# Two S4 convolutions mixed by a gate: fine magnitudes read by DVE from PSUM in every fifth table step instead of every third, in a new order

## The chip, the cores and the metric

The kernel runs on one core of one Trainium2 chip. A core has five engines that run at their own pace and meet at semaphores: PE (matrix multiplies), DVE (the vector engine), ACT (the scalar engine with its function tables), POOL (GpSimd, which cannot read PSUM) and SP, which issues transfers. The metric is the device time of one launch in microseconds; the time given is the median of three runs. A profile is one execution, recorded by the hardware, with its own time.

## The reference

The input `u` has 2048 positions and 512 channels. Two state-space layers A and B, each with 128 complex states per channel, turn it into two outputs, and a gate mixes them:

```python
g = sigmoid((x * gate_w).sum(-1, keepdims=True))
def layer(u, A_re, A_im, B_re, B_im, C_re, C_im, log_dt, Dskip):
    dt = exp(log_dt)[:, None]
    logdA, dB = dt * (A_re + 1j * A_im), dt * (B_re + 1j * B_im)
    P = exp(logdA[:, :, None] * l[None, None, :])          # 512 x 128 x 2048
    K = einsum("dn,dnl,dn->dl", C_re + 1j * C_im, P, dB).real
    y = irfft(rfft(u, 2 * L) * rfft(K, 2 * L))[:L] + u * Dskip
return g * layer_A(x) + (1 - g) * layer_B(x)
```

The sum over l of complex exponentials gives each channel a filter K of 2048 taps, and the layer is a causal convolution with it. Everything is float32.

## The kernel before, in words

The 512 channels are cut into 8 blocks of 64; with layers A and B side by side a block has 128 channel rows. The work has four parts.

*Preparation* (`prep`, `exp_dt`, `seed`, `seed_angles`): per state and channel the logarithm, the angle and the weight are worked out, and from these the *seeds*. The exponential over 2048 positions is split in two factors, fine and coarse, and each factor in two short lists: `ml` holds eight magnitudes for single positions (columns 0 to 7) and eight for steps of 8 (columns 8 to 15), `mh` the same for coarse steps, `sa` the angles as integers. ACT fills `ml` and `mh` with exponentials of the logarithm (line 523), once for each block; POOL makes the angles (lines 535 to 541).

*Tables* (`tables(T)`, 64 steps, T = 0 to 63, eight to a block, 16 channel rows each). A step has

- on POOL, the angles `ang`: two operations of 128x512 integers (lines 549 and 552);
- the *fine magnitudes*: `mr[:, :, 0:64]`, 128x1024, the outer product of the two halves of `ml` (lines 555 to 565). This is what the change is about;
- on POOL (or DVE), the *coarse magnitudes* `mr[:, :, 64:96]`, 128x512, from `mh` (line 566);
- on ACT, a sine of the angles, a sine of the half angles and a square (lines 570 to 572);
- on DVE, four products that turn these into the real and imaginary tables `mr` and `ei` (lines 573 to 579);
- on PE, 128 small multiplies, `kgen` (line 588), that sum over the states and give the filter's taps, and a copy into `kt` by ACT or DVE. Every second step adds the skip weight (POOL) and runs the first stage of the transform of the filter, `first` (line 605), with two copies into `xa` or `xb`.

In two of three steps the fine magnitudes are one operation on POOL, or on DVE where the order says so; both inputs are in SBUF. In the third, when `T % 3 == 2`, ACT first copies the eight seeds of each row (128x128) into a PSUM bank of the ring `c` (line 558), and DVE multiplies that by the other half of `ml` (line 559), so that one of its inputs comes from PSUM.

*Convolutions* (`conv`, `back`): for each block, eight times a second transform stage on PE (line 618) and a product with the transform of the input on DVE (line 690), and after every two of these an inverse stage on PE (line 710), two copies and a round trip through memory in another layout. *Finish* (`fin`): the last stage with the gate folded in (line 742), a copy, and a store.

All helpers record operations in a `Plan`; nothing is issued while they run. `ORDER` (lines 82 to 150) is a list, written out in the file, of the numbers of these operations: it sets in which sequence they are issued, and so each engine's queue. A number with `b` takes the second engine of those that an operation allows: DVE instead of ACT for a copy (`"act dve"`), DVE instead of POOL for an operation marked `any` (`"pool dve"`), POOL instead of SP for a store. Lines 269 to 298 are helpers that many operations share, so the profile has products under L271 and L281, activations under L284, copies under L294 (ACT) and L296 (DVE).

Buffers are rings: `mr` has three, `ang`, `ei` and `kt` two, `c` four PSUM banks; a ring's next buffer is the one whose last use stands earliest in the order. An engine that comes to an operation whose buffer is still in use waits, and everything behind it in its queue with it.

Of the kernel before, what the change touches and what calls it, by code (L numbers as in the profile page):

```python
# [82 lines left out]
6 7 11 8 9 4 2 182 3 1 82 83 0 84 475 86 186 183 18 19 20 24 21 22 23 25 26 27 28 29 30 31 32 33 34 35 37 88 184b 185b 38 17  # L83
36 85 190 326 40 44 45 39 41 42 46 47 48 366 76 49 50 51 59 79 73 71 75 187 52 53 188 189 54 55 56 57 138 58 191 193b 61 62
67 63 60 68 192 64 69 91 14 351 87 13 218 194 15 16 98 65 70 92 93 101 94 95 89 96 43 72 66 353 77 354 78 90 74 100 99 195
102 357 104 103 105 219 113 197b 196b 198 200 355 356 221b 114 360 358 359 199 201 385 203 205 386 361 107 204 206 106 220
226 127 222 327 202 207 210 213 208 209 211 212 129 80 97 12 368 369 383 367 81 10 384 362 108 363 109 110 111 215 214 370
364 216 365 223 112 116 115 371 224 373 122 121 117 123 374 225 372 388 124 118 119 120 387 375 227 217 1403 230 125 126 128
131 134 376 228 389 136 133 231 352 132 137 135 130 5 1406 229 429 232 377 233b 244 390 378 245 391 392 393 249 394 251 395
430 250b 397 398 399 400 401 246 402 403 479 247 477 476 480 478 141 396b 404 405 406 142 143 239 144 252b 145 146 248 1414  # L90
253 148 149 234 150 151 152 407 254 240 431 416 414 427 415 154 139 140b 153 235b 155 236 418 408 379 419 420 409 237 483 417
421 422 428 410 445 446 447 147 448 241 242 156 157 432 380 381 423 159 424 435 158 436 411 433 434 437 413b 438 382 412 160
458 459 481 255 262 175 238 258 484 449 450 257 256 425 439 161 163 452 451 426 440 485 460 482 441 461 162 259 165 166 260
261 453 172 171 173 174 454 263 462 463 265b 167 164 455 168 169 612 611 464 264 609 613 177 266 179 243 176 328 330 331 290
329b 465 267 269b 268b 466 456 457 610 487 467 468 280 282 281b 469 283b 488 470b 294 284 486 170 180 499 501 616 489 502 490
491 492 471 500 442 493 518 519 516 517 494 472 444 443 503 504 495 496 506 332 275 505 473 474 531 333 507 508 520 521 509
276b 497 510 498b 522 511 532 523 524 529 533 530 277 285 278 287 270 272 286 534 535 288 525 526 536 547 549 550 548 512 537
538 334 335 608 279 289 527 336 551 539 540 552 271 553 560 562 561 554 555 528b 541 337 273 564 542 513 563 556 339 178 338
557 558 579 514 515 567 568 580 565 559 566 581 577 543 578 582 593 591 592 594 1407 1408 569 570 585 1404 544 586 583 546
584 545 340 587 588 1405 595 596 341 571 572b 598 342 1415 1426 614 618 615 573 619 599 1416 597 1425 617 181 1417 1409 1410  # L100
1411 274 1412 589 633 590 622 623 349 345 1427 600 1418 1419 601 574 602 575 576 624 603 620 621 649 347 343 625 634 626 1420
1429 635 631 632 651 652 604 348 650 744 1421 636 637 681 1428 1436 1450 1437 1422b 627 1430 628 1438 639 640 605 629 638 607
606 630 653 1413 1423 1424 1447 1439 1431 654 641 642 655 1432 643 656 657 658 662 663 664 665 666 644 679 680 645 659 695
667 1433 668 1448 660 1440 669 670 1449 682 1441 684 685 661 683 693 671 672 687 344 350 694 696 346 646 647b 1442 688 1443b
1444b 1434 1458 741 742 746 648 686 673 1459 745 674 743 1451 1435 1445 1461 689 690 691 1460 1452 692b 712 710 675 711 713
676 697 698 700 1453 701 699 678 677 714 1454 715 1455 1462 702 1446 703 717 704 1757 1763 705 725 1463 718 726 716 1764 1758
1483 1469 1470 719 723 727 724 747 751 749 706 753 754 748 752 728 729 1464 720 1471 1465b 750 1759 1765 1456 1480 1472 1466b
721 1760 1766 731 1761b 876 730 732 733 722 1767 1481 1473 878 755 707 1482 734 1474 735 708 783 709 756 757 736 1762 1457
1768 1475 1484 764 766 765 737 767 758 784 759 760 768 1476 769 1477 738 761 771 1485 740b 739b 772 770 773 1491 1467 1494
1468 1478 1502 762 1486 1487b 1488b 774 1495 1496 877 874 875 1492 1503 1493 775 785 781 795 814 782 796 815 786 763 787 776  # L110
# [3 lines left out]
835 836 810b 837 850 811 1776 848 851 1779b 856 857 849 838 852 879 858 839 883 859 880 853 860 885 886 861 1528 1519 882  # L114
1501 854 1529 862 1520 855b 863 864 1521 1010 840 884 887 897 899 900 898 1780 1777 1522 842 841b 865 1530 866 1531b 1532b
888 889 291 292 890 867 868 293 891 892 901 295 893 894 297b 296 902 869 914 916 915 904 917 870 905 903 871 872 1538 1523
298 299 918 302 1533 1534 1512 906 895 301b 907 303 921 922 305b 908 927 928 919 300 920 896b 304b 929 932 933 909 316 306
308 923 924 930 307b 309b 931 945 946 947 910 318 1784 925 935 317b 1785b 936 926b 1781 1007 934 1008 319 1009 1011 1782 977
310 937 938 978 323 321 322b 939 1786 320 1783 324b 325 1535 1006 1546 948 949 952 940b 958 959 960 961 1014 941 979 950 313
311 1790 1787 951 953 312 314 1791 962 954 975 976 911 955 965 1788 963 966 913 964 912 1539 1536 956 1540 967 989 968 942  # L120
957 980 943 981 982 1537 944b 983 991 990 1547 1548 984 1550 1541 985 1542b 986 1543b 315 1015 1549 1571 1557 1789 969 1551
1558 987 1144 1143 970b 993 1016 1012 1013 992 971 994 1559 988 995 996 997 998 972 974 973 1552 1031 1017 1020 1553 999 1032
1018 1554 1544 1560 1582 1033 1019 1029 1000 1021 1001 1561 1023 1024 1562 1572 1002 1030 1003 1022 1034 1025 1026 1573 1037
1035 1036 1005 1004 1027 1569 1047 1049 1048 1050 1060 1038 1545 1555 1579 1568 1792 1139 1556 1028 1051 1052 1563 1564 1565
1039 1040 1054 1583 1041 1053 1042 1062 1061 1043 1063 1093 1077 1094 1055 1570 1574 1580 1064 1065 1056 1067 1057 1575b
1576b 1044 1068 1584 1581 1046b 1566 1590 1140 1141 1066 1069 1142 1045 1058 1591 1059 1079 1070 1080 1592 1091 1078 1081
# [3 lines left out]
1103 1128 1275 1182 1129 1606 1130 1131 1132 1802 1613 1602 1120 1803 1133 1603 1614 1134b 1150 1104 1151 1162 1163 1152 1135  # L130
1164 1165 1153 1156 1154 1105 1801 1615 1589 1155 1107 1106 1157 1183 1179 1180 1158 1136 1607 1166 1137 1167 1138b 1169 1159
1170 1225 1608 1609 1168 1600 1623 1637 1610 1271 1616 1160 1624 1617 1184 1226 1625 1171 1618 1185 1273 1172 1619b 1620 1635
1173 1187 1634 1804 1188 1161b 1186 1272 1174b 1636 1276 1274 1626 1621 1611 1193 1227 1194 1195 1175 1196 1210 1211 1627
1176 1189 1190 1628 1191 1197 1178b 1200 1198 1177 1199 1629 1192b 1630 1631 1638 1201 1622 1648 1645 1202 1639 1203 1646
1811 1212 1213 1214 1215 1216 1812 1640 1641 1632 1670 1647 1217 1218 1219 1204 1649 1642 1220 1650 1223 1279 1224 1241 1242
1228 1231 1232 1229 1230 1814 1805 1808 1205 1809 1233 1243 1244 1254 1255 1656 1643 1813 1221 1245 1222 1246 1815 1206 1256
# [698 lines left out]
```

## Time and profile before

| | |
|---|---|
| median of three runs | 480.89 us (473.8, 480.89, 481.37) |
| the profiled execution | 472.5 us |
| its span, from first to last instruction | 470.7 us |
| granted TensorE clock, mean | 0.971 |
| fine magnitudes on POOL (`mr<-ml`) | 43, 1960 ns each |
| fine magnitudes on DVE out of PSUM (`mr<-c,ml`) | 21, 1214 ns each |
| seed copies on ACT (`c<-ml`) | 21, 281 ns each |
| loads of ACT's function tables | 31, 1283 ns each |

A line of the profile names the line of code, the engine, the operation and, by the program's names, what is written from what. "Idle before" is the time in which that engine stood still ahead of such instructions, with what ended it. The chain of work is followed back from the last instruction, at each step to what released it. Consecutive instructions of an engine overlap somewhat, so a duration is longer than what the instruction adds to a full queue.

### The profile page before, as it was taken

Reading aid. Unit: us, or ns where it says so; the run is one execution under the profiler, and the core shown is the slowest. Engines: PE = TensorE matmul, PEld = TensorE weight load, DVE = VectorE, ACT = ScalarE, POOL = GpSimd, SP = SyncE. Lnnn points to the kernel's source line nnn. Section 1 sums busy time; section 2 is a strip of 40 time slices with the busy share of each in tenths; the row PEclk is TensorE's granted clock in tenths of the full one; section 3 lists DMA queues with packets and bytes.
Section 4 is the critical chain, followed back from the end, with each engine's and each line's share of the span. In section 5 each row is a group of like instructions: output and inputs, shape, how many; then the busy total and the mean of one; then the engine's idle time right before and its main releaser. Section 6 shows DMA issues by size and latency. Waiting matters only on the chain.

```text
span 470.7 us, 21838 instructions
## 1 busy us (share of the span) xinstructions
PE 394.9 (84%) x9616; PEld 356.4 (76%) x9616; DVE 416.0 (88%) x518; ACT 386.2 (82%) x676; POOL 338.8 (72%) x317
## 2 busy tenths in 40 slices
PE   4797786799968879998898988879598888999935
PEld 3786685689857768787798977778587877898934
DVE  6999889999999999999899999998789999996610
ACT  3889979999988999998899999998789898791110
POOL 2593859599977989796999689878929899650010
PEclk9899899999998999999999999999999999999987
DMA  7866852836555565876465646764838667567793
GB/s 220 276 198 205 246 161 78 249 120 224 183 157 157 133 160 180 212 206 178 132 180 153 206 132 190 193 182 117 195 105 218 167 192 213 152 184 187 212 244 89
DMA packets 74542, 84.53 MB, mean 180 GB/s; under 512 B 5456, under 2 KB 60112, under 8 KB 73392
## 3 DMA queue, kind: packets, MB, share of 16 engines
q1 hardware_dynamic: 74304, 82.75, 62.0%
q8 instruction: 75, 1.23, 1.1%
q0 software_dynamic: 144, 0.39, 0.3%
q14 instruction: 19, 0.16, 0.1%
HBM read 51.48 MB, written 31.65 MB: 177 GB/s over the span
## 4 chain that ended last, share of the span: by engine, by line
PE 35%; DVE 25%; ACT 21%; issue 11%; DMA 4%; SPq 3%; DVEq 0%; POOL 0%; ACTq 0%
PE c L618 8%; PE c L605 8%; DVE mr L281 6%; PE c L588 6%; PE c L742 5%; PE c L710 4%; DVE y L690 4%; ACT s L284 4%; DVE ei L271 4%; ACT ang L284 3%; ACT sq L284 3%; SPq L289 3%; ACT ml L523 2%; DVE ei L281 2%; PE c L439 2%
## 5 line engine op out<-in xcount | busy, mean ns | idle before, releaser
L281 DVE SCALAR_TENSOR_TENSOR mr<-sq,mr 128x1024 f32<-128x1024 f32 (+1 forms) x128 | 117.4, 947 | 1.9 <-ACT sq L284 1.5
L271 POOL TENSOR_TENSOR mr<-ml 128x1024 f32<-128x1024 f32 x43 | 84.3, 1960 | 12.3 <-PE c L588 7.7
L271 POOL TENSOR_TENSOR ang<-par,cint 128x512 int32<-128x512 int32 x64 | 67.5, 1055 | 31.0 <-ACT sq L284 15.9
L271 DVE TENSOR_TENSOR ei<-s,mr 128x1024 f32<-128x1024 f32 x64 | 77.7, 1214 | 4.1 <-ACT s L284 2.8
L588 PE MATMUL c<-mr 128*32 128x64 f32 x2048 | 64.7, 223 | 14.8 <-DVE mr L281 7.3
L605 PE MATMUL c<-small,kt 128*64 128x128 f32 x1024 | 66.3, 283 | 10.9 <-issue 5.0
L690 DVE TENSOR_TENSOR y<-c,u 128x1024 f32<-128x1024 f32 x57 | 68.7, 1214 | 4.3 <-PE c L618 1.7
L284 ACT ACTIVATE s<-ang 128x1024 f32<-128x1024 int32 x64 | 65.9, 1029 | 6.5 <-POOL ang L271 4.5
L605 PEld LDWEIGHTS c<-small,kt 128*64 128x64 f32 x1024 | 58.2, 141 | 15.4 <-issue 6.3
L271 POOL TENSOR_TENSOR mr<-mh 128x512 f32<-128x512 f32 x63 | 67.7, 1080 | 2.4 <-PE c L588 2.4
L271 POOL TENSOR_TENSOR ang<-sa 128x512 int32<-128x512 int32 x64 | 68.6, 1073 | 0.2
L284 ACT ACTIVATE ang<-ang 128x1024 f32<-128x1024 int32 x64 | 67.7, 1058 | 1.2
L284 ACT ACTIVATE sq<-ang 128x1024 f32<-128x1024 f32 x64 | 66.0, 1032 | 3.2 <-DVE mr L281 2.3
L588 PEld LDWEIGHTS c<-mr 128*32 128x32 f32 x2048 | 48.6, 110 | 25.5 <-issue 9.9
L588 PE MATMUL c<-ei 128*32 128x64 f32 x2048 | 64.1, 221 | 3.2 <-issue 3.2
L710 PE MATMUL c<-y,vv 64*64 64x128 f32 x1792 | 59.9, 274 | 4.6 <-issue 2.7
L710 PEld LDWEIGHTS c<-y,vv 64*64 64x64 f32 x1792 | 50.9, 134 | 10.6 <-issue 5.2
L618 PE MATMUL c<-xa,w 128*128 128x128 f32 x384 | 52.8, 287 | 3.5 <-DVE vv L414 1.3
L618 PE MATMUL c<-xb,w 128*128 128x128 f32 x384 | 50.0, 282 | 4.7 <-DVE xb L296 1.3
L588 PEld LDWEIGHTS c<-ei 128*32 128x32 f32 x2048 | 50.6, 111 | 3.6 <-issue 3.6
L618 PEld LDWEIGHTS c<-xa,w 128*128 128x128 f32 x384 | 46.4, 194 | 7.7 <-issue 3.6
L618 PEld LDWEIGHTS c<-xb,w 128*128 128x128 f32 x384 | 45.1, 191 | 8.5 <-issue 3.1
(109 smaller groups left out, 661.9 us busy)
## 6 DMA issues: line engine op xcount, KB each, us to landing
zb<-z SPq DMA_DIRECT2D x31, 512.0 KB, 3.9
u<-us SPq DMA_DIRECT2D x57, 256.0 KB, 4.4
f<-zb SPq DMA_DIRECT2D x28, 512.0 KB, 5.2
us<-z SPq DMA_DIRECT2D x16, 512.0 KB, 3.7
uin<-in_uk_dram SPq DMA_DIRECT2D x16, 256.0 KB, 3.9
f<-in_ut_dram SPq DMA_DIRECT2D x8, 512.0 KB, 5.3
out_dram<-o SPq DMA_DIRECT2D x29, 128.0 KB, 3.2
par<-prd SPq DMA_DIRECT2D x7, 320.0 KB, 3.9
```

The source lines that it names most:

```text
L271: lambda e: (dve if e == "dve" else pool).tensor_tensor(out=out(), in0=in0(), in1=in1(), op=o),
L281: lambda _: dve.scalar_tensor_tensor(out=out(), in0=in0(), scalar=s, in1=in1(), op0=o0, op1=o1), reads, writes, port=port)
L284: op("act", "act", n, lambda _: act.activation(out=out(), in_=in_(), func=func, **{k: v() if callable(v) else v for k, v in kw.items()}), ...
L289: lambda e: (sp if e == "sp" else pool).dma_start(out=out(), in_=in_()), reads, writes, touch=touch)
L439: pe.matmul(t(*ps)[:, CH * i:CH * i + CH], V(x)()[:, CH * i:CH * i + CH], dgv()[:, k, i], start=True, stop=True)
L523: act.activation(out=t(*tile)[:, ks, j], in_=t("par", c)[:, 0, ks].bitcast(F32), func=AF.Exp, scale=float(l))
L588: pe.matmul(ps[32 * j:32 * j + 32, o], x[:, 4 * o + j, 64:96], x[:, 4 * o + j, 0:64], start=part == 0, stop=part == 1, tile_position=(0, 3 ...
L605: pe.matmul(t(*ps[g // 4])[64 * r:64 * r + 64, 128 * (g % 4):128 * (g % 4) + 128], t(*x)[:, g], t("small")[:, 128 * r:128 * r + 128], star ...
L618: pe.matmul(view()[:, :, k], t("w2", j // 2)[:, 4 * (j % 2) + k], t(*x1)[:, 4 * j + k], start=True, stop=True)
L690: op("dve", "tt1", 1024, lambda _: dve.tensor_tensor(out=t(*y).rearrange("p h s f d -> p h s (f d)"), in0=fv().rearrange("p s f d -> p s ( ...
L710: pe.matmul(bank_of(x)[64 * e:64 * e + 64, CH * q:CH * q + CH], v[:, 0:64] if h else v[:, 32:96], t(*ys[f // 4])[64 * x:64 * x + 64, h, :, ...
L742: pe.matmul(t(*ps)[64 * r:64 * r + 64, DC * i:DC * i + DC], t("gsi")[:, 4 * k + i, s, 64 * r:64 * r + 64], t(*f)[:, 8 * k + 2 * i + r, DC ...
```

## The change

The condition in `tables` is `T % 5 == 4` instead of `T % 3 == 2`. So 12 steps instead of 21 take the way through PSUM: 4, 9, 14 and so on to 59. The other 52 have the operation marked `any`. Nine seed copies fall away, the operations are 1844 instead of 1853, and their numbers shift, so `ORDER` is written anew as a whole; it is a different sequence, not the old one with numbers mapped.

```diff
 ORDER = """
-6 7 11 8 9 4 2 182 3 1 82 83 0 84 475 86 186 183 18 19 20 24 21 22 23 25 26 27 28 29 30 31 32 33 34 35 37 88 184b 185b 38 17
...
+10 11 6 12 4 2 182 0 186 16 83 82 3 1 5 183 18 19 20 21 22 23 25 26 27 28 29 24 30 31 32 33 34 17 35 37 185 36 184 88 40 44
...
 """
@@
         tt("pool", G * 32, lambda: t(*A)[:, :, 32:64].rearrange("p c (h l) -> p c h l", l=4),
...
-        if T % 3 == 2:
+        if T % 5 == 4:
             sd = ("c", "seeds", T)
             few = lambda: t(*sd)[:, 0:8 * G].rearrange("p (c h) -> p c h", h=8)
             actv(8 * G, few, lambda: t(*ml)[:, k:k + G, 8:16], AF.Copy, [ml + q], [sd])
```

What the two lists assign differently, counted from them: of the 52 fine magnitudes marked `any`, the new list gives 51 to POOL and one, step 11, to DVE (before: 43, all POOL); the coarse magnitudes are all POOL's (before: step 55 was DVE's). Copies of 256 elements: 69 on ACT and 27 on DVE (before 73 and 23). Copies of 512 elements: 138 and 59 (before 140 and 57). In ACT's queue the function table changes 28 times (before 30). Uses of a bank of the ring `c`: 381 (before 390). PE's operations and the transfers are the same in number and size.

More of the change, by code (lines that the diff above doesn't have):

```diff
@@ L87 @@
[L87 to L90, printed above, removed]
@@ new lines @@
+210 361 114 108 109 113 362 363 81 385 369 383 386 80 384 226 222 202 207 327 370 209 211 212 129 110 214 215 216 111 217 125
+364 365 112 223 116 115 371 225 224 372 373 374 121 122 117 123 124 118 119 120 396 397 398 399 227 230 126 127 135 128 131
+130 132 352 134 136 1405 137 375 231 229b 376 387 388 232 228 377 378 389 233b 244 245 249 246 251 390 391 392 393 400 401
+402 250b 247b 252b 394 148 141 144 478 479 476 475 477 395b 403 404 405 406 142 143 145 149 139 146 133 1397 151 140b 407 253
@@ new lines @@
+869 737 1485 1459 771 1487 1469 1477 1478b 1479b 1483 1484 870 871 873 780 791 781 792 793 794 1497 1494 785 1495 1488 783
+1496 1480 1504 1507 772 1498 1489b 786 784 773 774 877 808 809 810 1490 795 787 1508 775 788 1509 798 799 789 796 777 797 790
+1499 812 776 1500 813 1501 800 801 1470 1515 1505 1516 814 1506 1517 802 1481 1760 1763 1766 841 811 839 815 816 821 822 842
+1761 803 823 826 817 1764 818 824 827 825 804 840 829 828 830 1518 1491 1762 1765 1502 1529 1769 819 1770 820 843 805 831
@@ new lines @@
+1767b 844 832 846 833 845 806 834 852 854 853 879 855 835 875 876 1510 1519 847 848 849 856 807b 857 850 1511b 878 1005 858
+1512b 1520 851b 859 860 1492 1513 1771 836 861 838 837 880 883 291 1521 862 293b 292b 863 1522b 911 1523 295 884 864 892 881
+882 912 886 913 893 885 887 865 894 895 909 910 1768 1503 298 302 297 296 896 888 866 299 889 868b 867 897 303 898 300 301
+899 900 1526 1524 1525 1514 890 901 902 304b 914 305 915 891b 917 918 923 1527 924 916 321 306 903 322 927 323 919 307b 1528
@@ new lines @@
+1062 1040b 1052 1063 1133 1135 1053 1134 1073 1039b 1064 1074 1576 1075 1072 1085 1086 1140 1088 1076 1568 1584 1065 1585
+1077 1078 1577 1066 1079 1080 1578 1089 1569 1132 1592 1595 1579 1787 1788 1090 1586 1081 1082 1104 1067 1068 1102 1105 1103
+1091 1092 1093 1083 1784 1094 1070 1106 1069 1095 1785 1107 1108 1084 1109 1596 1587 1096 1115 1116 1117 1118 1142 1110 1597
+1111 1119 1588 1097 1589 1120 1157 1112 1122 1790 1141 1603 1789 1606 1786 1590 1793 1113 1121 1791 1123 1158 1794b 1124 1125
@@ new lines @@
+1593 1114b 1594 1604 1126 1605 1127b 1268 1138 1139 1143 1098 1144 1145 1155 1128 1156 1159 1146 1099 1149 1580 1147 1148
+1150 1100b 1101 1129 1151 1598 1160 1130 1161 1131 1599 1152 1163 1164 1607 1608 1591 1614 1795 1264 1615 1153 1173 1174 1218
+1600 1162 1177 1175 1186 1176 1187 1616 1154b 1165 1166 1609 1610b 1178 1617 1601 1625 1618 1626 1266 1611 1619 1627 1180
+1179 1181 1629 1167 1620 1269 1168 1267 1265 1621 1628 1612 1636 1182 1637 1622b 1630 1183 1638 1203 1188 1219 1169 1170
+1172b 1272 1204 1189 1613 1602 1184 1190 1191 1193 1194 1192 1171 1195 1185 1207 1196 1205 1206 1210 1211 1631 1208 1209 1632
@@ new lines @@
+1377 1365 1368 1369 1370 1371 1378 1379 1695 1358 1817 1808 1372 1696 1359 1381 1382 1809 1686 1380 1360 1373 1374 1384 1818
+1383 1687 1385 1688 1386 1375 1361 1387 1376b 1363 1668 1388 1692 1389b 1362 1693 1679 1689 1819 1810 1690 1390 1391 1697
+1393b 1392 1698b 1699 1706 1707 1703 1714 1717 1704 1708 1700 1727 1701 1715 1718 1709 1710b 1725 1728 1719 1739 1736 1729
+1726 1730 1737 1740 1711 1720 1721 1722 1712 1829 1741 1826 1820 1823 1742 1743 1824 1830 1731b 1732b 1733 1723 1744 1745
+1734 1746 1831b 1825 1827b 1821 1747 1828b 1822 1835 1832 1836 1833 1837 1834 1838 1841 1839 1842 1840b 1843
```

82 lines of the change are left out of this document (31 added, 51 removed), and 19 rows, old and new, of the table ORDER.

## The prediction

> **What bounds the kernel now.** I read the page from the busy shares down: first which engine is fullest, then in which stretch, then what that engine waits for there.
>
> ```profile
> PE 394.9 (84%) x9616; PEld 356.4 (76%) x9616; DVE 416.0 (88%) x518; ACT 386.2 (82%) x676; POOL 338.8 (72%) x317
> ```
>
> DVE is the fullest engine, but an average hides stages. The table of busy time by stretch (length, PE, PEld, DVE, ACT, POOL, clock, DMA share, GB/s) shows them:
>
> ```profile
> 60.00:120.00 60.00, 51.47 (x1055) 46.06 (x1058) 58.93 (x74) 54.94 (x94) 47.92 (x44) 1.00 0.56 174
> 120.00:180.00 60.00, 49.36 (x1246) 43.17 (x1237) 58.68 (x67) 55.83 (x91) 52.56 (x47) 0.97 0.54 154
> 180.00:240.00 60.00, 55.69 (x1532) 49.89 (x1530) 57.80 (x67) 55.56 (x96) 51.74 (x47) 1.00 0.66 180
> 240.00:320.00 80.00, 71.24 (x1832) 65.23 (x1828) 78.60 (x94) 76.27 (x135) 67.64 (x63) 0.98 0.62 172
> 320.00:360.00 40.00, 32.71 (x924) 29.24 (x922) 32.99 (x38) 34.62 (x65) 29.30 (x26) 0.96 0.65 163
> 360.00:420.00 60.00, 54.11 (x1592) 48.62 (x1588) 57.38 (x64) 51.53 (x78) 52.78 (x48) 1.00 0.66 184
> 420.00:471.00 51.00, 36.48 (x887) 33.77 (x876) 21.77 (x26) 10.34 (x20) 2.22 (x5) 0.90 0.69 180
> ```
>
> From 60 to 420 us DVE works 58.93 + 58.68 + 57.80 + 78.60 + 32.99 + 57.38 = 344.4 of 360 us: 96%, with 15.6 us idle, 7.0 of them between 320 and 360. POOL works 301.9 there (84%), ACT 328.8 (91%), PE 314.6 (87%). So this stretch is DVE's, with ACT and PE close behind and POOL having the room. After 420 us DVE is idle more than half the time; the chain there is PE's last convolutions and then a round trip by DMA:
>
> ```profile
> 432.12 3.77 PE c L618 x32
> ...
> 451.16 5.34 DMA zb<-z
> 456.89 4.33 DMA xa<-zb
> ```
>
> The new order keeps the same operations in that tail, shuffled slightly, so I carry its 50 us over. What the stretch's engines wait for (us in total, times, longest), POOL first:
>
> ```profile
> POOL ang L271 <- ACT sq L284: 15.9, 11, 4.3
> POOL kt L271 <- ACT kt L294: 14.6, 7, 5.1
> POOL mr L271 <- PE c L588: 9.8, 6, 3.3
> ...
> DVE xb L296 <- PE c L605: 5.1, 1, 5.1
> DVE ei L271 <- ACT s L284: 2.8, 4, 1.8
> DVE mr L281 <- ACT sq L284: 1.5, 5, 0.6
> ...
> DVE mr L271 <- ACT c L284: 0.5, 1, 0.5
> ...
> ACT s L284 <- POOL ang L271: 4.5, 6, 1.8
> ```
>
> POOL mostly waits because it is ahead: for an angle or magnitude buffer that a later engine has not emptied. The one sign of POOL being late is ACT's 4.5 us for angles.
>
> **The change, part by part.** Single durations overlap their neighbours, so I price by the distance from one start to the next:
>
> ```profile
> 326.53 1.21 DVE L271 TENSOR_TENSOR mr<-c,ml 128x1024 f32<-128x1024 f32 x1
> 327.66 1.21 DVE L271 TENSOR_TENSOR ei<-s,mr 128x1024 f32<-128x1024 f32 x1
> ...
> 334.52 0.41 DVE L296 COPY kt<-c 128x256 f32<-128x256 f32 x1
> 334.90 1.23 DVE L271 TENSOR_TENSOR ei<-s,mr 128x1024 f32<-128x1024 f32 x1
> ...
> 329.84 1.96 POOL L271 TENSOR_TENSOR mr<-ml 128x1024 f32<-128x1024 f32 x1
> 331.76 1.05 POOL L271 TENSOR_TENSOR ang<-par,cint 128x512 int32<-128x512 int32 x1
> ...
> 323.03 0.28 ACT L284 ACTIVATE c<-ml 128x128 f32<-128x128 f32 x1
> 323.23 1.03 ACT L284 ACTIVATE sq<-ang 128x1024 f32<-128x1024 f32 x1
> 327.53 0.39 ACT L294 ACTIVATE kt<-c 128x256 f32<-128x256 f32 x1
> 327.80 1.05 ACT L284 ACTIVATE sq<-ang 128x1024 f32<-128x1024 f32 x1
> 328.86 1.28 ACT L523 ACT_TABLE_LOAD   x1
> ```
>
> A 1024-wide DVE multiply costs 1.13 us in a row of them, POOL's 1.92, a 256-wide DVE copy 0.38, the ACT copy of the seeds 0.20, ACT's 256-wide copy 0.27, a table load 1.28. Counting the two order lists by engine:
>
> DVE: 21 multiplies out of PSUM become 12, other steps than before among them, so nine go: 9 x 1.13 = -10.2. A tenth step, 11, stays on DVE but now reads SBUF twice, which adds one multiply. No such 1024-wide operation is in the trace; one 512-wide is:
>
> ```profile
> L271 DVE TENSOR_TENSOR mr<-mh 128x512 f32<-128x512 f32 x1 | 0.8, 769 | 0.0
> L296 DVE COPY z<-c 128x512 f32<-128x512 f32 x25 | 16.3, 679 | 0.3 <-PE c L710 0.3
> L294 ACT ACTIVATE z<-c 128x512 f32<-128x512 f32 x63 | 36.0, 596 | 12.0 <-PE c L710 9.3 <-PE c L618 2.7
> ```
>
> Its bounds are 1.13 (as from PSUM) and 2 x 0.77 = 1.54; I take 1.2, nearer the same width. That 512-wide coarse multiply itself (step 55) goes to POOL: -0.8. Four copies of 256 and two of 512 move from ACT to DVE: 4 x 0.38 + 2 x 0.65 (16.3 / 25) = +2.8. Sum for DVE: -10.2 + 1.2 - 0.8 + 2.8 = -7.0 us.
>
> POOL: eight more fine multiplies, 8 x 1.92 = 15.4, and one coarse, 1.0: +16.4 us.
>
> ACT: nine seed copies, 9 x 0.20 = -1.8; the six result copies, 4 x 0.27 + 2 x 0.57 (36.0 / 63) = -2.2; in the list the function table changes 28 times instead of 30, 2 x 1.28 = -2.6. Sum -6.6 us. I book nothing for it: ACT is behind DVE as the bound, and if DVE were not there to cover it, it would be worth up to 6.6.
>
> PE and DMA: the same instructions and transfers. Each seed copy also held one of the four 512-wide PSUM banks from ACT's copy to DVE's multiply; 390 bank uses become 381. That is 2% fewer; no row names a wait for it, and I price it at zero. What hides it is that DVE finds its seeds ready: it waited once, 0.5 us, which is the end on the side of a gain.
>
> A wait is added: where DVE fetched its own fine magnitudes, it now waits for POOL's. Behind a late POOL multiply on POOL stand its coarse multiply and the next step's angles; ACT's sine waits for those and DVE's product for both. In the stretch POOL goes from 301.9 of 360 to about 318 of 353 (both with the terms above), from 84% to 90%. Its ratio of busy to idle goes from 301.9/58.1 = 5.2 to 318/35 = 9.1; if the 4.5 us of lateness at ACT grow with it, they become 7.9, +3.4. I let two thirds of that reach DVE, since ACT's 9% of idle time takes up some and DVE already waits 2.8 + 1.5 us for ACT: an estimate of +2.2 us, with ends of 0 and the whole 16.4.
>
> Sum: -7.0 + 2.2 = -4.8 us. The profiled execution took 472.5 us around a span of 470.7; it becomes 467.7. The median of the three runs is 480.89 (473.8 to 481.37), 1.8% above the profiled one, so the same ratio gives 480.89 x 467.7 / 472.5 = 476.0 us. Which of the two levels a median lands on I cannot tell from the profile; it goes into the range.
>
> The rule that speaks against this change concerns the port that DVE and POOL share:
>
> ```profile
> L271 POOL TENSOR_TENSOR mr<-ml x43: 1943/1954/2181, 24.6 to 414.0; 128x1024 f32<-128x1024 f32 x43
> ...
> L271 DVE TENSOR_TENSOR ei<-s,mr x64: 1209/1212/1226, 28.8 to 421.3; 128x1024 f32<-128x1024 f32 x64
> ```
>
> Minimum, median and maximum hardly differ for either engine, though both are busy nearly all the time: neither blocks the other while DVE takes one operand from PSUM. The Trainium skill, Perfetto Trace Analysis, "Optimizing Scalar/DVE Operations", warns that because GpSimd and DVE share an SBUF port, moving work between them might not help. By that rule alone the sum would lose its gain; these rows do not bear it out, because the steady DVE operations are not of the locking kind. It is a rival below, with a small chance.
>
> **The rivals.**
>
> *More than the sum.* The largest single DVE wait stands before a copy of a first-stage result (step 47) that comes early in DVE's queue and late in PE's:
>
> ```profile
> 342.99 0.69 DVE L296 COPY xb<-c 128x512 f32<-128x512 f32 x1 [5.14 <-PE c L605]
> ```
>  In the new list both copies of step 47 are ACT's. If that stall goes and no other takes its place, the change is -7.0 - 5.1 = -12.1, and 480.89 x 460.4 / 472.5 = 468.6 us, 2.6% faster. For: the place is gone from DVE's list, and ACT and PSUM are eased. Against: ACT then waits there, and a new order has its own such places.
>
> *Hidden.* PE is 90% busy from 360 to 420 and is the chain from about 415 on; if it is PE that ends the last steps, DVE's gain becomes DVE idling: about 0, 480.9 us. For: that chain. Against: before 360 PE is at most 93%, and its idle time before the table matmuls is largely the wait for DVE:
>
> ```profile
> PE c L588 <- DVE mr L281: 7.3, 10, 1.9
> ```
>
> *POOL becomes the bound (slower).* Four POOL steps now follow one another. A step's angles and coarse magnitudes take about 3.1 us, the fine ones 1.92, four steps 20 us; where a new block of channels begins, POOL also computes its seeds:
>
> ```profile
> 322.62 2.83 POOL L271 TENSOR_TENSOR sa<-par,cint 128x1536 int32<-128x1536 int32 x1
> 325.52 1.10 POOL L271 TENSOR_TENSOR sa<-sa,par 128x512 int32<-128x512 int32 x1
> 326.58 1.11 POOL L271 TENSOR_TENSOR mh<-mh,par 128x512 f32<-128x512 f32 x1
> ```
>
> That is 5 us more, 25 us, against (421.3 - 28.8) / 63 x 4 = 24.9 us that four steps take now: the point from which POOL decides is just reached at the seven block starts. Should each expose its 2.83 us seed multiply, 7 x 2.83 = 19.8, less 7.0, is +12.8: 493.9 us, 2.7% slower. Against: POOL may run two steps ahead (two angle buffers), and it idled 58 us.
>
> *The port.* If each of the eight added POOL multiplies held DVE for its 1.92 us, +15.4 - 7.0 = +8.4: 489.4 us, 1.8% slower. The equal durations above speak against it.
>
> **How the numbers follow.** Forecast (-3 to -9 us on either level) 0.40; more than the sum 0.22; hidden 0.20; POOL bound 0.15; port 0.03. About 2%, 9.6 us, is what a measurement of this kernel can tell from no change. Faster by over 2%: 0.22. Slower: 0.15. Within: 0.63. The time is 476.0; the likeliest case's own range is 472 to 478 on the median's level and down to 464 on the profiled one's. For 8 in 10 I take 464 to 486: it holds the forecast, the gain of 12 us, no change, and part of the POOL cases; the slow ends are left out.
>
> **What would show it.** Right: DVE near 409 us busy, POOL near 355, ACT near 380; the wait of POOL for ACT's squares shorter than 15.9 us; DVE still over 94% from 60 to 420, that stretch some 5 us shorter; the tail of about 50 us as before. POOL bound: ACT's wait for angles well over 8 us, or DVE waiting for POOL's magnitudes in so many words. Port: DVE's product or POOL's multiply with a maximum far from its median. More than the sum: no DVE wait over 3 us between 60 and 420. Hidden: PE's idle in 360 to 420 nearly gone while DVE's grows. Wrong altogether I would be if the new order has a fresh stall of 5 us or more that the counts of work cannot show: I counted what stands in each queue, not when its inputs come.

## The result, and the profile after

The change makes the kernel slightly slower. The ratio of the times after and before, on the same chip, is 1.0078 with a 95% interval of 1.0051 to 1.0105. The medians of 20 runs each are 478.33 us after (475.16 to 487.87) and 475.38 us before (472.42 to 485.11). The three runs shown ahead of the prediction had a median of 480.89 us, so they lay high: with 20 runs the old kernel is at 475.38. The ratio compares, of each kernel, only the runs within 1.5% of its fastest, so it is not the quotient of the two medians. The profiled execution after took 477.64 us with a span of 475.8; the one before had 470.7, so the two profiles differ by 5.1 us.

First the busy time of each engine on the page of the changed kernel.

```profile
PE 396.4 (83%) x9616; PEld 359.1 (75%) x9616; DVE 408.9 (86%) x515; ACT 380.4 (80%) x659; POOL 354.2 (74%) x326
```

The work did move as counted: DVE lost 7.1 us (416.0 before), ACT 5.8, and POOL gained 15.4. Yet the time grew. The table by stretch of the changed kernel, with the columns of the one before (length, PE, PEld, DVE, ACT, POOL, clock, DMA share, GB/s), shows what became of the 7 us:

```profile
60.00:120.00 60.00, 52.25 (x1029) 46.59 (x1030) 58.96 (x76) 55.63 (x100) 47.35 (x45) 1.00 0.53 162
120.00:180.00 60.00, 51.54 (x1271) 45.90 (x1268) 59.09 (x67) 53.45 (x88) 54.84 (x48) 0.94 0.59 168
180.00:240.00 60.00, 51.39 (x1360) 46.96 (x1363) 50.27 (x59) 49.32 (x84) 47.60 (x42) 0.91 0.59 162
240.00:320.00 80.00, 72.75 (x1954) 66.59 (x1942) 78.50 (x95) 77.93 (x138) 73.69 (x67) 1.00 0.64 178
320.00:360.00 40.00, 36.00 (x1024) 32.81 (x1024) 37.41 (x45) 38.28 (x68) 36.88 (x33) 1.00 0.62 167
360.00:420.00 60.00, 50.36 (x1454) 45.09 (x1448) 53.31 (x62) 46.63 (x67) 53.17 (x48) 0.97 0.65 182
```

From 60 to 420 us DVE works 337.5 of the 360 us, so it is idle for 22.5; before it was idle for 15.6. The 6.9 us of work that it has lost there came back as 6.9 us of standing still. Most of the idle time sits in two places: 180 to 240 (9.7 us) and 360 to 420 (6.7 us). In both PE does less than before (51.39 and 50.36 us, against 55.69 and 54.11), and its clock is lower (0.91 and 0.97, against 1.00 and 1.00). The waits of the changed kernel from 60 to 420 us (total, times, longest) name PE too:

```profile
POOL ang L270 <- ACT sq L283: 17.9, 12, 4.2
...
DVE y L689 <- PE c L617: 10.8, 6, 6.0
...
PE c L709 <- issue: 6.2, 3, 4.1
...
PE c L587 <- issue: 5.2, 5, 3.3
...
ACT s L283 <- POOL ang L270: 2.2, 3, 1.0
```

ACT waits 2.2 us for POOL's angles, less than the 4.5 before, so by the waits POOL is not late. It is not out of the way either. In the chain of work that ended last, before and after, POOL's share goes from nothing to 10% and that of the transfers from 4% to 12%:

```profile
PE 35%; DVE 25%; ACT 21%; issue 11%; DMA 4%; SPq 3%; DVEq 0%; POOL 0%; ACTq 0%
```

```profile
PE 30%; DVE 21%; ACT 12%; issue 12%; DMA 12%; POOL 10%; SPq 1%; DVEq 0%; ACTq 0%; POOLq 0%
```

Both are taken up below. What is new is DVE's wait for PE's second transform stage, 10.8 us (1.0 before), and behind it PE's waits for "issue", which is time in which PE waited for nothing that the profile shows. The largest of these, with PE's timeline of the changed kernel around it (start, length, what, count):

```profile
203.83 1.95 PE L617 MATMUL c<-xa,w 128*128 128x128 f32 x16
...
213.40 1.41 PE L709 MATMUL c<-y,vv 64*64 64x128 f32 x41
218.86 1.55 PE L709 MATMUL c<-y,vv 64*64 64x128 f32 x23 [4.05 <-issue]
220.35 3.78 PE L617 MATMUL c<-xa,w 128*128 128x128 f32 x16
```

And DVE's timeline of the same kernel at that place:

```profile
222.46 1.23 DVE L689 TENSOR_TENSOR y<-c,u 128x1024 f32<-128x1024 f32 x1 [6.04 <-PE c L617]
```

PE stops for 4.05 us after 41 of the 64 multiplies of a group. The 64 belong to one operation with one set of inputs, all present, and no semaphore stands between the 41st and the 42nd. After the pause 16 multiplies of the next stage take 3.78 us, where 16 of them took 1.95 at 203.83: the granted clock, in the windows below, has fallen to half. DVE stands still for 6.04 us. What the transfers do meanwhile is in the windows of the changed kernel around the pause:

```profile
210.00:214.00 4.00, 3.64 (x119) 3.27 (x121) 4.00 (x5) 3.97 (x7) 3.79 (x5) 1.00 1.06 268
214.00:219.00 5.00, 0.95 (x33) 0.81 (x29) 2.41 (x4) 1.87 (x4) 5.00 (x4) 0.82 0.86 220
219.00:224.00 5.00, 5.00 (x39) 4.50 (x38) 1.23 (x1) 2.94 (x4) 0.82 (x2) 0.50 0.03 8
```

The DMA share is 1.06 ahead of the pause, 0.86 in it and 0.03 behind it: PE goes on as the transfers drain. One of the queues carries instructions. In the changed kernel's transfers from 205 to 219 us (packets, MB, share) it gets two packets:

```profile
q1 hardware_dynamic: 2823, 3.33, 88.9%
q8 instruction: 2, 0.03, 1.1%
```

Over the whole run this queue moves 75 packets of 16 KB. PE has 9616 multiplies and 9616 weight loads, 19,232 instructions, which is about 256 for each packet; from 60 to 420 us there are 62, one every 5.8 us.

I call a stop of 0.9 us or more between two multiplies of one group, with no semaphore between them, a *pause*. After the change there are seven, 15.0 us together; before there were five, 9.2 us. Set beside the single records of the instruction queue, each of the twelve ends 1.3 to 1.5 us after a packet of instructions has landed (times in us, from the records of the two traces):

```
         PE stops   packet starts, lands   PE goes on   after landing
before      80.74       79.30    80.76        82.17        1.41
           156.02      155.21   156.29       157.76        1.47
           233.72      232.26   233.43       234.76        1.33
           335.77      337.07   338.43       339.79        1.36
           424.58      423.03   424.17       425.54        1.37
after      188.86      187.08   188.61       189.89        1.28
           214.81      215.98   217.35       218.86        1.51
           331.72      330.30   331.18       332.67        1.49
           339.16      337.62   338.96       340.33        1.37
           360.38      358.95   360.33       361.87        1.54
           379.91      380.77   381.83       383.24        1.41
           427.24      427.44   428.81       430.25        1.44
```

Packets come every 5.8 us, so that twelve of twelve hit the same quarter of a microsecond is no chance. The places say the same. Count all of PE's instructions in the two traces, those of its sequencer included (19,373 before, 19,363 after): at each of the twelve pauses, the number that have started is k x 256 + 193 for some whole k, and the packet that PE then goes on with is the k-th to land. So each pause stands where one packet ends and the next begins: PE has run out of instructions and waits for the next packet. In the four long ones, of 3 to 4 us, the packet's transfer does not even start until PE has stopped. Why it starts late the table does not say; that the DMA engines are full of data is the theory that the experiments test. The old kernel's longest pause is one that the prediction met without knowing it. Its own PE timeline:

```profile
333.51 2.26 PE L605 MATMUL c<-small,kt 128*64 128x128 f32 x36
339.79 3.16 PE L605 MATMUL c<-small,kt 128*64 128x128 f32 x28 [4.02 <-issue]
```

This is the group that DVE's copy at 342.99 waited 5.14 us for, the stall that the prediction put down to the order of the queues.

The limit of 0.9 us flatters the old kernel, which has many shorter stops. All of PE's waits for "issue" from 60 to 420 us sum to 15.1 us after the change, in 12 places. Before, they sum to 14.3 us, in 16 places, and all 16 stand at the end of a packet. The two largest rows of the old kernel are:

```profile
PE c L605 <- issue: 5.4, 2, 4.0
...
PE c L588 <- issue: 4.0, 5, 1.7
```

So in this stretch the new kernel hardly loses more time to missing instructions than the old one; it loses it in fewer and longer stops. What does grow there is the time at half clock, 10.2 us before and 20.7 after by the clock records of the traces.

The time from the first table product on DVE to the last closes the account. Before it was 421.3 - 28.8 = 392.5 us. The rows of the same tile in the changed kernel:

```profile
L270 DVE TENSOR_TENSOR ei<-s,mr x64: 1206/1214/1226, 28.8 to 423.9; 128x1024 f32<-128x1024 f32 x64
```

That is 395.1 us, 2.6 more; what comes after grows from 49.4 to 51.9 us, 2.5 more, and a pause of 3.02 us at 427.2 (0.96 at 424.6 before) lies in it. Together these are the 5.1 us of the two spans.

### The profile page after: what moved, and what is told of

The parts are those of the page before. It is cut to its first block, busy times and chain, and to the rows that moved or that the text cites. A ratio compares the mean times of both kernels' runs of the same rounds, so it can differ in the third digit from the quotient of the medians.

```text
span 475.8 us, 21831 instructions
## 1 busy us (share of the span) xinstructions
PE 396.4 (83%) x9616; PEld 359.1 (75%) x9616; DVE 408.9 (86%) x515; ACT 380.4 (80%) x659; POOL 354.2 (74%) x326
## 4 chain that ended last, share of the span: by engine, by line
PE 30%; DVE 21%; ACT 12%; issue 12%; DMA 12%; POOL 10%; SPq 1%; DVEq 0%; ACTq 0%; POOLq 0%
PE c L604 7%; PE c L617 5%; PE c L587 5%; POOL mr L270 5%; DVE mr L280 5%; PE c L709 4%; PE c L741 4%; DMA zb<-z 4%; DVE ei L270 3%; DVE y L689 3%; POOL ang L270 3%; DMA gsi<-in_pk_dram 3%; ACT s L283 2%; DMA f<-zb 2%; ACT sq L283 2%
## 5 line engine op out<-in xcount | busy, mean ns | idle before, releaser
L270 POOL TENSOR_TENSOR mr<-ml 128x1024 f32<-128x1024 f32 x51 | 99.6, 1954 | 5.2 <-ACT s L283 2.5
L270 POOL TENSOR_TENSOR ang<-par,cint 128x512 int32<-128x512 int32 x64 | 67.3, 1051 | 34.8 <-ACT sq L283 20.7
L587 PE MATMUL c<-mr 128*32 128x64 f32 x2048 | 65.9, 226 | 13.9 <-DVE mr L280 5.7
L604 PE MATMUL c<-small,kt 128*64 128x128 f32 x1024 | 64.7, 278 | 8.4 <-issue 4.2
L587 PEld LDWEIGHTS c<-mr 128*32 128x32 f32 x2048 | 49.4, 112 | 24.9 <-issue 15.5
L587 PE MATMUL c<-ei 128*32 128x64 f32 x2048 | 65.7, 223 | 1.9 <-issue 1.9
L604 PEld LDWEIGHTS c<-small,kt 128*64 128x64 f32 x1024 | 56.9, 138 | 12.4 <-issue 5.4
L709 PEld LDWEIGHTS c<-y,vv 64*64 64x64 f32 x1792 | 52.1, 138 | 12.4 <-issue 6.9
L587 PEld LDWEIGHTS c<-ei 128*32 128x32 f32 x2048 | 51.7, 113 | 2.2 <-issue 2.2
```

The source lines that it names most:

```text
L270: lambda e: (dve if e == "dve" else pool).tensor_tensor(out=out(), in0=in0(), in1=in1(), op=o),
L587: pe.matmul(ps[32 * j:32 * j + 32, o], x[:, 4 * o + j, 64:96], x[:, 4 * o + j, 0:64], start=part == 0, stop=part == 1, tile_position=(0, 3 ...
L604: pe.matmul(t(*ps[g // 4])[64 * r:64 * r + 64, 128 * (g % 4):128 * (g % 4) + 128], t(*x)[:, g], t("small")[:, 128 * r:128 * r + 128], star ...
L709: pe.matmul(bank_of(x)[64 * e:64 * e + 64, CH * q:CH * q + CH], v[:, 0:64] if h else v[:, 32:96], t(*ys[f // 4])[64 * x:64 * x + 64, h, :, ...
```

## The experiments

The ratios are to the kernel before on the same chip, with 95% intervals. The diffs show only the core of each edit.

### Does POOL pay for the move?

*e1* keeps the old sequence and moves nine of the 21 multiplies to POOL in place, each ahead of its step's coarse multiply; their seed copies go.

```diff
-        if T % 3 == 2:
+        if T % 3 == 2 and T not in (8, 14, 20, 26, 32, 38, 44, 50, 56):
```

> The sequence of before is kept; nine of its 21 steps with fine magnitudes from PSUM (8, 14, 20, ... 56) get theirs from POOL, issued just ahead of the step's coarse magnitudes, and their nine seed copies fall away. Theory A (the move is worth some 5 us, but the new order has more pauses of PE inside its groups, 15 us of them against 9): ratio to before 0.985 to 0.992. Theory B (POOL becomes the bound, in whatever order): 1.00 to 1.02. Theory C (DVE's busy time does not set the time at all): 0.997 to 1.003.

Measured: 1.0062 (1.0007 to 1.0118). That misses the range of theory A and lies in that of B; C's range, up to 1.003, meets the interval. It costs about as much as the whole change, so alone it does not show what the new order does.

*e2* takes DVE's side alone: in the old kernel nine multiplies out of PSUM are cut to a sixteenth of their width, and the products of those steps read `ml` where they would read the missing magnitudes. *e3* does the same to eight of POOL's multiplies in the new kernel.

```diff
+        m = 1 if T in (8, 14, 20, 26, 32, 38, 44, 50, 56) else G
...
-            tt("dve", G * 64, lambda: t(*M)[:, :, 0:64].rearrange("p c (h l) -> p c h l", l=8),
+            tt("dve", G * 64, lambda: t(*M)[:, 0:m, 0:64].rearrange("p c (h l) -> p c h l", l=8),
```

> Before, with nine of the 21 DVE multiplies (the same nine steps) cut to one of 16 rows and nothing put on POOL; the products of these steps read other magnitudes, so the output is not the reference's. Takes some 9 x 1.06 = 9.5 us from DVE. If DVE is the bound between 60 and 420 us: ratio 0.979 to 0.986. If a loop through PE, ACT and POOL sets the pace (C): 0.995 to 1.00.

> After, with eight of the POOL multiplies that the change added (steps 8, 17, 23, 32, 38, 47, 53, 62) cut to one of 16 rows; the products of these steps read other magnitudes, so the output is not the reference's. Takes some 8 x 1.8 = 14 us from POOL and leaves the order as it is. B (POOL bound): at least 5 us less than after, ratio to before 0.997 or less. A or C: as after, 1.005 to 1.011.

Measured: e2 1.0053 (1.0014 to 1.0092), e3 1.0125 (1.0067 to 1.0183). Less work and more time: the edits had added a wait. The exponentials that fill `ml` for a later block now had to wait for DVE's last read of it. The waits of e2 from 60 to 420 us show it:

```profile
ACT L523 <- DVE mr L281: 4.4, 1, 4.4
```

Both missed their ranges, and both say nothing of DVE or POOL. *e9* and *e10* repeat them, partly in other steps, with the products reading a constant tile (`vv`), which is not overwritten any more.

> Before, all transfers whole, nine of the 21 DVE multiplies (steps 17, 20, 26, 32, 35, 41, 47, 50, 56) cut to one of 16 rows; the products of these steps read a constant tile in place of the magnitudes (in the first run of this kind they read the seeds, and ACT's next seeds waited 4.4 us for them in one place; that wait can't arise here); the output is not the reference's. If DVE's time is worth its length: ratio 0.979 to 0.986. If PE's pauses take it back: 0.99 to 1.005.

> After, all transfers whole, eight of the POOL multiplies (steps 17, 23, 26, 32, 38, 41, 47, 53) cut to one of 16 rows, 14 us off POOL; the products read a constant tile; the output is not the reference's. POOL bound (B): 1.000 or less. POOL not the bound: 1.003 to 1.012.

Measured: e9 0.9953 (0.9895 to 1.001), e10 1.012 (1.0029 to 1.0212). The 21 multiplies, nine of them cut, take 16.5 us in place of 25.5, and that moves the time by less than can be told from zero; at most 1%, 5 us. In e9's profile the pauses sum to 13.6 us, so they may have taken some of it back; e11 below is free of most of them. Taking 12.9 us of POOL's work away from the new kernel (354.2 to 341.3) does not make it faster than the new kernel is (1.0078); the interval leaves room for 0.5%. So, although the chain runs over POOL, the amount of POOL's work is not what bounds the new kernel.

### Are the pauses the transfers' doing?

*e4* (new kernel) and *e5* (old kernel) move fewer bytes with the same instructions, waits and order: for all blocks but the last the loads of `f` bring a quarter, and the loads of `u` half, and the multiplies and products read what is there again, so this part of the output is computed from other data.

```diff
-            m = NA // (1 + end)
+            m = NA // (1 + end) if last else 8
...
-        dma(256, lambda: uv().rearrange("p h f d -> p (h f d)"),
+        dma(256, lambda: uv()[:, 0].rearrange("p f d -> p (f d)"),
```

> After, with the loads of the filtered block before the last stage cut to a quarter (all blocks but the last) and the loads of the input's spectrum cut to half; the same transfers, waits and order otherwise; the output is not the reference's. A (PE's pauses come from its instruction fetches standing behind data in the DMA engines): pauses inside PE's groups fall below 5 us in the profile and the ratio to before to 0.995 or less. B or C: 1.003 to 1.011.

> Before, with the same smaller loads as in the run of after with fewer bytes (0.968 of before); the output is not the reference's. A (the move and the new order are worth their 5 to 7 us of DVE time, but pauses of PE took them back): 0.976 to 0.985, that is 4 to 8 us slower than after with fewer bytes. C (DVE's time is not what sets the pace, pauses or not): 0.964 to 0.972, the same as after with fewer bytes.

Measured: e4 0.9682 (0.9632 to 0.9733), e5 0.9815 (0.9772 to 0.9858). With fewer bytes the new kernel is the faster one, by 1 - 0.9682 / 0.9815 = 1.4%, and the intervals do not touch. First the new, then the old kernel with fewer bytes, from 60 to 420 us in one window:

```profile
60.00:420.00 360.00, 320.47 (x8428) 288.76 (x8429) 348.44 (x413) 330.62 (x560) 317.77 (x283) 0.99 0.42 127
```

```profile
60.00:420.00 360.00, 320.33 (x8360) 287.51 (x8360) 352.04 (x410) 332.72 (x564) 303.02 (x272) 0.99 0.42 127
```

The DMA share is 0.42 for both (0.61 with whole transfers). Of the pauses the new kernel keeps one of 1.1 us, the old one two, 2.7 us together; the time at half clock in this stretch falls to 6.8 us in the new kernel and 4.4 in the old one. PE's waits for "issue" in e4 from 60 to 445 us are down to these:

```profile
PE c L741 <- issue: 1.1, 1, 1.1
...
PE c L709 <- issue: 0.7, 1, 0.7
...
PE c L587 <- issue: 0.3, 1, 0.3
```

They were 18.1 us in the new kernel and 15.3 in the old one. Smaller transfers also land sooner, which would help in another way, and the chain of the new kernel runs over transfers twice in this stretch, some 20 us, where the old one's does not. But from 60 to 420 us all waits of the engines ended by data transfers sum to 4.4 us in the new kernel (the largest 2.0) and 1.0 in the old one, far less than the 19 us between the medians of the new kernel and of e4 (459.25). What these few us are worth was not tested apart.

*e6* (new) and *e7* (old) change no byte: 32 small multiplies, in the trace 64 multiplies and 64 weight loads and so 128 instructions, are put into PE's stream ahead of the first tables, half a packet. *e16* (new) puts in 64, a whole packet.

```diff
+            for _ in range(32 * (name == ("u", 0, 1))):
+                pe.matmul(t(*ps[1])[64:128, 384:400], t(*x)[:, 7], t("small")[:, 128:144], start=True, stop=True, tile_position=(0, 64))
```

> After, with 32 more small matmuls on PE at about 13 us, where it waits anyhow (they repeat the last one of a group into the same bank, so the result is the same): PE's instruction stream is shifted against its fetches, and nothing else is changed. If pauses of PE from late fetches cost time, they move to other places and the time changes with their sum, by up to 1% either way (0.995 to 1.015). If the pauses do not matter: as after, 1.008 within 0.002.

> Before, with the same 32 matmuls. If the pauses cost time and before had been fortunate in where they fell: 1.003 to 1.015. If they do not matter: 1.000 within 0.002.

> After, all transfers whole, with 64 more small matmuls on PE at about 13 us (32 gave 1.004, none 1.008). If the sum of PE's pauses sets the difference to before: anywhere from 0.994 to 1.015, going with the sum of the pauses in its profile. If the first shift's change was chance: 1.006 to 1.010.

Measured: e6 1.0039 (0.9983 to 1.0095), e7 1.008 (1.0039 to 1.0121), e16 1.0338 (1.0277 to 1.0399). These times carry the padding itself, since the first table product starts later than at 28.8 us: by 3.8 in e6, 2.8 in e7, 10.3 in e16, which also takes e16 out of both its ranges. The places are what counts. With half a packet the pause of 4.05 us is gone, and the group of 64 runs through in 1.98 us; e6 has three others, 5.6 us together. With a whole packet five of the seven are back at the same multiplies (the other two are down to 0.5 us, and one of 1.3 us is new). The group of 64 breaks again after the 41st, in e16's PE timeline:

```profile
221.15 1.41 PE L711 MATMUL c<-y,vv 64*64 64x128 f32 x41
226.04 1.56 PE L711 MATMUL c<-y,vv 64*64 64x128 f32 x23 [3.48 <-issue]
```

So where a pause falls follows the place of the instruction in its packet. From the first to the last table product e6 takes 388.9 us and e7, the old order with the same padding, 387.8:

```profile
L270 DVE TENSOR_TENSOR ei<-s,mr x64: 1206/1215/1225, 32.6 to 421.5; 128x1024 f32<-128x1024 f32 x64
```

```profile
L271 DVE TENSOR_TENSOR ei<-s,mr x64: 1207/1214/1226, 31.6 to 419.4; 128x1024 f32<-128x1024 f32 x64
```

The pauses from 60 to 420 us and this stretch go together in both orders. In the new one they are 12.0 us and 395.1, in e16 10.8 and 394.4, in e6 4.1 and 388.9, in e4 (fewer bytes) 1.1 and 380.6; in the old one 8.2 and 392.5, in e7 3.1 and 387.8, in e5 (fewer bytes) 2.7 and 383.8. That e6 is a faster kernel is not shown: with its padding it is not told from the old one. Nor is it faster than e7 in this stretch, where all of PE's waits for "issue" sum to 7.4 us in both; e6 has 19.4 us at half clock there, e7 9.3. So the sum of the stops does not account for the difference between the two orders.

### Without the pauses: who carries the chain?

The base is now e5, which keeps 2.7 us of pauses. *e8* cuts the nine DVE multiplies as e2 does, *e11* as e9 does; *e12* is e4 with POOL relieved as in e10; *e13* is e1 with fewer bytes.

> Before with the smaller loads and with nine DVE multiplies cut to one of 16 rows (9.5 us off DVE); the output is not the reference's. If DVE is the bound once PE no longer pauses: 5 to 9 us, 0.011 to 0.019, below before with the smaller loads alone. If it is not the bound even then: the same within 0.003.

> Before with the smaller loads (0.9815 of before) and nine DVE multiplies cut as in the run with whole transfers. If DVE is the bound once PE no longer pauses: 0.965 to 0.972 (5 to 8 us off). If it is not: 0.978 to 0.984.

> After with the smaller loads (0.968 of before) and eight POOL multiplies cut as in the run with whole transfers. If POOL had become the bound underneath the pauses: 0.955 to 0.962. If POOL has room: 0.965 to 0.970.

> The old order with nine fine multiplies moved to POOL (1.006 of before with whole transfers), with the smaller loads; the output is not the reference's. If the gain of after with fewer bytes (0.968 to 0.970 against 0.9815) is the move's: 0.967 to 0.973. If it is the new order's: 0.978 to 0.985.

Measured: e8 0.993 (0.9897 to 0.9963), which has the wait shown above for e2 and is set aside; e11 0.9802 (0.9737 to 0.9867); e12 0.9701 (0.9646 to 0.9756); e13 1.0016 (0.9991 to 1.004).

e11 against e5 (0.9815): 8.3 us of DVE's busy time (415.9 to 407.6), 1.7% of the time, are worth 0.1%; the two intervals leave room for up to 0.9%, half of it. The stretch from the first to the last table product is no shorter, 384.5 us against 383.8. DVE then waits for ACT instead, in e11 from 60 to 420 us:

```profile
DVE mr L281 <- ACT sq L284: 5.1, 10, 1.3
...
DVE ei L271 <- ACT s L284: 3.3, 6, 1.0
```

In e5 these were 1.9 and 0.9 us. e12 against e4 (0.9682): no gain is seen from taking POOL's added work away in the new order, though POOL has 15% of the chain in e4 (3% in e5); the intervals leave room for some 0.6%. But e13, above both its ranges, is 2% slower than e5: the same move in the old order makes POOL late, as e13's waits from 60 to 420 us show:

```profile
ACT s L283 <- POOL ang L270: 11.5, 9, 2.3
...
DVE ei L270 <- ACT s L283: 7.7, 8, 3.0
...
DVE ei L270 <- POOL mr L270: 5.5, 5, 1.6
```

e4 has 3.5, 1.7 and 0.9 us there. So the move alone loses, and the new order, with the few operations that it gives to other engines, wins it back and more: e4 is 3.3% faster than e13. That it does so by sending POOL's work earlier is what the shorter waits suggest; it was not tested apart.

*e14* takes ACT's side on the base of e5: nine squares are cut to one column and their readers take the sine's bank. *e15* adds the DVE cut of e11.

```diff
+        short = T in (17, 20, 26, 32, 35, 41, 47, 50, 56)
+        sq = lambda: t(*S) if short else t(*Q)
...
-        stt(G * 64, lambda: t(*M)[:, :, 32:96], lambda: t(*Q), 1.0,
+        stt(G * 64, lambda: t(*M)[:, :, 32:96], sq, 1.0,
```

> Before with the smaller loads; in nine steps (17, 20, 26, 32, 35, 41, 47, 50, 56) ACT's square is cut to one of 16 rows and the products read the sine in its place, about 9 x 0.9 = 8 us off ACT and a shorter way from the angles to the products; the output is not the reference's. If ACT sets the pace without pauses: 0.963 to 0.972. If DVE, ACT and PE hold each other: 0.977 to 0.983.

> The same with nine DVE multiplies cut in the same steps as well. If DVE and ACT bound together: 0.962 to 0.970 and clearly below both runs in which one of them is relieved. If PE or something else bounds: 0.976 to 0.983.

Measured: 0.9975 (0.9928 to 1.0022) and 0.9927 (0.9886 to 0.9969), both slower than e5. The sine's bank is now held until the last product, and ACT's next sine waits for it, in e14 from 60 to 420 us:

```profile
ACT s L284 <- DVE mr L281: 9.6, 5, 3.0
```

Both are set aside. *e17* relieves ACT without a new reader: in blocks 2, 3, 5 and 6 two of every five exponentials are left out, and their readers find older values. *e18* adds the DVE cut.

```diff
-                    for tile, j, l in some:
+                    for tile, j, l in some[:3] if c in (2, 3, 5, 6) else some:
```

> Before with the smaller loads (0.9815 of before); in blocks 2, 3, 5 and 6 two of every five of ACT's exponentials are left out, so the seeds of these columns are old ones and the output is not the reference's. 40 exponentials less, about 40 x 0.27 = 11 us off ACT. If ACT sets the pace: 0.960 to 0.970. If no engine alone does: 0.976 to 0.983.

> The same, with nine DVE multiplies cut to one of 16 rows as well (steps 17, 20, 26, 32, 35, 41, 47, 50, 56, their products read a constant tile; that alone gave 0.980). If DVE and ACT bound together, which is what after relieves: 0.962 to 0.971. If PE or a latency around the engines bounds: 0.975 to 0.983.

Measured: e17 0.9749 (0.9692 to 0.9805), e18 0.9731 (0.9667 to 0.9794). Both lie between the ranges that were set for them. ACT's 7.5 us (385.1 to 377.6) give some 0.7%, DVE's on top 0.2%, with intervals that overlap e5's in both. Neither engine is seen to hold the chain alone, and relieving both gives some 0.9%, 4 us, for 7 us off DVE and 8 off ACT.

## Why the prediction was wrong

The range, 464 to 486, held 478.33. The direction, a gain of 4.8 us, was wrong: by the ratio the change costs 0.8%, some 3.7 us.

*The sum for DVE, -7.0 us*, was taken as time. The size was right: DVE 408.9 busy (409 forecast), and POOL 354.2 (355) and ACT 380.4 (380) as well. The step that failed is the one before it: "So this stretch is DVE's". That DVE is 96% busy does not make its work the length of the stretch when ACT has 91%, PE 87%, and each waits for the others in order. e11 shows it with most of the pauses gone: 8.3 us of busy time fewer, 0.1% of time, and a stretch no shorter. In its place DVE waited for ACT's single sines and squares, 8.4 us instead of 2.8. So about half of such a gain, at the least, is not to be had even with few pauses.

*PE and DMA: "the same instructions and transfers".* The sum has no term for PE's stops or for its clock. The rows of the stops were there before: from 60 to 445 us PE waited for "issue" 6.4 us at L605 and 4.0 at L588 in the old kernel, and this was not read. With the order, the place of each packet's end against the bursts of transfers changes. From 60 to 420 us the stops grow only from 14.3 to 15.1 us in sum, but they become longer. The stretches at half clock go from three of 3.4 us to one of 6.8 and four of 3.4, of which two stand behind pauses of over 3 us, and this takes up to 3 x 1.7 = 5.1 us more from PE. Behind 420 us a pause of 0.96 us becomes one of 3.02, 2.1 more. That is up to 0.8 + 5.1 + 2.1 = 8.0 us, an estimate, against the 10 us by which the change turns from a gain of 1.4% (e4 against e5) to a loss of 0.8%.

*More than the sum: the largest single DVE wait.* The 5.1 us stall was read as a copy "early in DVE's queue and late in PE's". It was a pause of PE in the middle of a group. It did go, and another, of 6.04 us, came, behind a pause of its own. The text named this case last: "a fresh stall of 5 us or more that the counts of work cannot show".

*POOL's lateness, +2.2.* Wrong for the new order, where ACT's wait for angles fell from 4.5 to 2.2 us; right in kind, and too small, for the move by itself (e13, 2%). *ACT, -6.6, booked at nothing*: 5.8 measured, and it should not have been nothing if DVE's counted in full; ACT's is worth no less than DVE's as far as e17 and e11 can tell (0.7% and 0.1%).

*The port.* Refuted as forecast: with eight more of them, POOL's multiply still takes the same time in the changed kernel.

```profile
L270 POOL TENSOR_TENSOR mr<-ml x51: 1941/1951/2133, 25.7 to 419.2; 128x1024 f32<-128x1024 f32 x51
```

*The marks.* DVE 93.8% from 60 to 420, not over 94; that stretch not 5 us shorter but 2.6 longer; POOL's wait for squares not shorter than 15.9 us but 17.9. The tail was 51.9 us for "about 50".

*The level.* Scaling to 480.89 put the forecast at 476.0; on the later median of 475.38 the same sum would be 470.6, so the near hit is luck.

What is shown is that DVE's time was not worth its length. What stays open is the rest of the loss. That PE waits for instructions is shown by the table and the count; that the packets start late because of the data is inferred from the full DMA engines at the long pauses and from their going with fewer bytes. The pauses were never taken away with all else left alone, so how much of the loss is theirs, how much the half clock's and how much that of transfers that land later was not separated.

## What to carry to other kernels

Where three engines are over 85% busy in one pipeline, the busy time taken off the fullest one is not the forecast; cut its work in an experiment first, and check in the waits that the cut has added no new reader to a buffer. Read the waits for "issue" of the engine with the most instructions: a stop in the middle of a group is no matter of the queue's order, and a new order can move such stops, and make them fewer and longer, without any change in the work. Sum all of them before you call them more: a limit of 0.9 us showed 8.2 and 12.0 us here where the whole sums are 14.3 and 15.1. And judge a move of work and the order written for it apart: here, with small transfers, the move alone costs 2% and its order wins 3.3%, and neither could be seen with whole ones.

## What the runs showed of the hardware

PE can stand still for up to 4.05 us in the middle of a group of multiplies whose inputs are all present, while data transfers keep the DMA engines full (share 1.06 ahead of it). With the share at 0.42 instead of 0.61, the pauses of the new kernel fall from 15.0 to 1.1 us and those of the old one from 9.2 to 2.7. Each of twelve pauses ended 1.3 to 1.5 us after a packet of 16 KB, 256 instructions, had landed, and stood where one packet ends.

Behind the longest pause 16 multiplies took 3.78 us instead of 1.95. The Trainium skill, TensorE: Matmul & The Clock Gate, "What's actually happening", says that the clock falls to half after an idle window of about 3.4 us and returns after a busy one. The trace agrees in the length of the steps, with half the clock from 217.3 to 224.1 us, two such windows; but the clock fell 2.4 us after PE had stopped, and PE had worked 1.0 us of the 3.4 us before that.
